# Block differences moved from GpSimd to VectorE, and a hand-written order made anew with other costs

## Chip, core and metric

The kernel runs on one core of one Trainium2 chip. The metric is the device time of one execution in microseconds (us); the median of three runs counts. Engines are called by their short names: PE (TensorE), DVE (VectorE), ACT (ScalarE), POOL (GpSimd) and SP (the queue that issues every DMA here).

## What is computed

```python
# q, k, v: (8, 8, 576, 64): attention inside chunks of 64 tokens, per head
scores = (q_c @ k_c^T) / 8; attn = softmax(scores); x = attn @ v_c
x = x as 4608 tokens x 512
h = relu(x @ moe_w_in)            # 512 x 2048
x = (h * h) @ moe_w_out           # 2048 x 512
gate = sigmoid(x @ moe2_w_gate); val = x @ moe2_w_val      # 512 x 1536 each
out = (gate * val) @ moe2_w_out   # 1536 x 512
```

All weights come as float64 and are made float32 on the chip.

## The kernel before

All four products are done in float32 exactness by three passes of a reduced format: each operand is split into a high part (one ACT copy) and a low part (one DVE subtraction, line 447, `out = value - high`, both in SBUF). Each 2x2 block product is done in Strassen's manner with seven products P1 to P7 instead of eight, so operands are first subtracted from each other. The order of the program is:

1. Attention of 36 tiles of 128 tokens (lines 816 to 914) beside the product with w_in: matmuls of line 649 with 384 columns.
2. The product with w_out (line 1031, 384 columns), class `Long`: for each of six token pairs the seven products, each over eight weight groups. For one group PE does six matmuls; ahead of it stand one low-part subtraction on DVE and, in P5, P6, P7 and P4, one block subtraction (line 456) of the tiles `g` that were loaded from DRAM.
3. The products with w_gate and w_val (line 649, 512 and 256 columns).
4. The last product (line 1031, 512 and 256 columns), class `Long` again, over six weight groups, with tiles `u` in place of `g`.

Class `Long` takes a table `engines` that says for each of the four differences which engine does it; what the table doesn't name goes to POOL:

```python
for oo, xx, yy in zip(o, x, y):
    binary(self.engines.get(p, "POOL"), self.words(oo), self.words(xx), self.words(yy), ALU.subtract,
           self.n, [oo], {oo, xx, yy})
```

Weights are prepared on the way (lines 489 to 512 turn float64 into float32: two steps on ACT, three on DVE at lines 496, 498 and 505, and one addition on POOL at line 512; `wf` and `w` are such weights). Sums of weight blocks (`ws`, `sums`) and differences of token blocks of products 1 and 3 (`raw`, `yr`) are POOL's, line 456.

Nothing of this stands in the order in which it is written. Every piece is a job with an engine, a cost, its inputs and outputs; class `Plan` walks through time with these costs, gives out SBUF space and PSUM banks, takes on each engine the ready job with the earliest due time, and emits the instructions in the order that it found. So a cost changes no instruction, but the place of many in each engine's queue, which is worked off in order. A job marked `shared` is one whose DVE or POOL instruction has its inputs in SBUF alone. `cost(eng, n)` gives the cost of one instruction over n columns; the table `TIMES` gives, for each attention tile, when its PE steps (turning k and q, scores S, turning T, mixing X) are due.

## Time and profile before

| | us |
|---|---|
| median of 3 runs (1633.62 to 1635.81) | 1635.25 |
| the profiled execution | 1635.46 |
| its span, first to last instruction | 1633.7 |
| PE busy | 1599.7 (98%) |
| DVE busy | 1376.7 (84%) |
| ACT busy | 974.6 (60%) |
| POOL busy | 817.1 (50%) |

The profile is of one execution; 1.8 us of its time lie outside the span. An engine counts as busy from the start of an instruction's record to its end, so time in which an instruction is held up by another engine counts as busy too.

### The profile page before, as it was taken

To read this page: it belongs to the slowest core of one execution; us is meant where nothing else is said; L and a number is where in the kernel's file an instruction comes from. 1 tells how busy PE (TensorE), PEld (TensorE's weight loads), DVE (VectorE), ACT (ScalarE), POOL (GpSimd) and SP (SyncE) were. 2 spreads that over 40 slices of the span, in tenths; PEclk is the share of its full clock that TensorE was granted. 3 is DMA by queue.
4 is the path that set the end of the run, shared out by engine and by line. 5 is a ranking of instruction groups with operands and counts; after the bars stand their busy time and mean duration, and the time that the engine had idled before them with its cause. 6 is when DMAs were issued, how large, how long until landed. Compare 5 with 4: busy or idle time off the path is not lost.

```text
span 1633.7 us, 30814 instructions
## 1 busy us (share of the span) xinstructions
PE 1599.7 (98%) x10500; PEld 1445.2 (88%) x10500; DVE 1376.7 (84%) x2074; ACT 974.6 (60%) x1968; POOL 817.1 (50%) x636
## 2 busy tenths in 40 slices
PE   7999999999999999999999999999999999999998
PEld 5998998999899999999997898888888888877887
DVE  7998877788889999999999796755777858799996
ACT  7876666676676566565565565544555545545543
POOL 1253403030534544544479695644666647387672
PEclk8999999999999999999999999999999999999999
DMA  9864565877884665685687746487536578866572
GB/s 229 224 184 131 143 182 151 214 196 219 265 274 153 224 204 181 197 260 182 214 274 243 273 148 217 168 282 265 185 138 243 186 248 253 273 194 159 162 179 46
DMA packets 390798, 333.36 MB, mean 204 GB/s; under 512 B 234736, under 2 KB 325616, under 8 KB 390640
## 3 DMA queue, kind: packets, MB, share of 16 engines
q1 hardware_dynamic: 390640, 331.38, 66.5%
q8 instruction: 83, 1.36, 0.4%
q14 instruction: 75, 0.61, 0.1%
HBM read 209.13 MB, written 122.16 MB: 203 GB/s over the span
## 4 chain that ended last, share of the span: by engine, by line
PE 84%; DVE 9%; DMA 2%; issue 2%; ACT 1%; POOL 1%; SPq 1%; DVEq 0%; POOLq 0%; ACTq 0%
PE bank L649 46%; PE bank L1031 35%; PE bank L836 1%; PE bank L816 1%; PE bank L896 1%; DMA wraw__1337<-in_moe_w_in_dram 1%; PE bank L880 1%; SPq L420 1%; DMA gd<-c__4078 0%; DMA v__9966<-ad 0%; DMA k__299<-in_k_dram 0%; POOL ws__7533 L456 0%; DMA k__4752<-in_k_dram 0%; POOL wf__7203 L512 0%; DMA ud<-s__10228 0%
## 5 line engine op out<-in xcount | busy, mean ns | idle before, releaser
L512 POOL TENSOR_TENSOR wf__3400<-wf__3400,wr__3217 128x512 int32<-128x512 int32 x16 | 21.9, 1372 | 160.5 <-DVE wf__3400 L505 56.3
L512 POOL TENSOR_TENSOR wf__7203<-wf__7203,wr__6924 128x512 int32<-128x512 int32 x18 | 25.3, 1406 | 88.0 <-DVE wf__7203 L505 19.6
L512 POOL TENSOR_TENSOR wf__7000<-wf__7000,wr__6924 128x512 int32<-128x512 int32 x18 | 27.2, 1510 | 62.2 <-DVE wf__7000 L505 38.9
L456 POOL TENSOR_TENSOR raw__510<-raw__679,raw__510 128x384 f32<-128x384 f32 x20 | 24.4, 1240 | 55.6 <-DVE B__640 L447 23.3
L493 ACT ACTIVATE wr__6924<-wr__6924 128x512 int32<-128x512 uint32 x36 | 23.8, 662 | 0.0
L447 DVE TENSOR_TENSOR wx__7711<-ws__7533,wx__7711 128x512 fp32r<-128x512 f32 x18 | 17.7, 983 | 3.3 <-ACT wx__7711 L442 3.3
L447 DVE TENSOR_TENSOR wx__7143<-ws__7533,wx__7143 128x512 fp32r<-128x512 f32 x18 | 18.6, 1035 | 0.3 <-ACT wx__7143 L442 0.3
L496 DVE TENSOR_SCALAR wf__7203<-wf__7203 128x512 f32<-128x512 f32 x18 | 9.9, 549 | 9.6 <-ACT wf__7203 L489 9.6
L498 DVE TENSOR_SCALAR wf__7203<-wf__7203 128x512 int32<-128x512 int32 x18 | 17.4, 968 | 0.6
L489 ACT ACTIVATE wf__3400<-wr__3217 128x512 f32<-128x512 f32 x16 | 10.7, 666 | 11.3 <-DMA wf<-wf__3400 11.3
L456 POOL TENSOR_TENSOR ws__7533<-wf__7000,wf__7203 128x256 f32<-128x256 f32 x18 | 16.5, 915 | 1.3 <-DVE wx__7711 L447 1.1
L456 POOL TENSOR_TENSOR ws__7533<-ws__7533,wf__7000 128x256 f32<-128x256 f32 x18 | 15.8, 877 | 1.2
L512 POOL TENSOR_TENSOR w__670<-w__670,wraw__566 128x512 int32<-128x512 int32 x1 | 1.3, 1289 | 29.5 <-DMA wraw__645<-in_moe_w_in_dram 29.5
L447 DVE TENSOR_TENSOR wx__7485<-wf__7203,wx__7485 128x256 fp32r<-128x256 f32 x18 | 13.3, 737 | 3.1 <-ACT wx__7485 L442 3.1
L496 DVE TENSOR_SCALAR wf__7000<-wf__7000 128x512 f32<-128x512 f32 x18 | 9.8, 544 | 6.2 <-ACT wf__7000 L489 6.2
L498 DVE TENSOR_SCALAR wf__7000<-wf__7000 128x512 int32<-128x512 int32 x18 | 14.2, 791 | 0.6
L505 DVE SCALAR_TENSOR_TENSOR wf__7203<-wr__6924,wf__7203 128x512 int32<-128x512 int32 x18 | 14.5, 807 | 0.2
L489 ACT ACTIVATE wf__7000<-wr__6924 128x512 f32<-128x512 f32 x18 | 11.9, 660 | 4.3 <-POOL ws__7533 L456 4.3
L505 DVE SCALAR_TENSOR_TENSOR wf__7000<-wr__6924,wf__7000 128x512 int32<-128x512 int32 x18 | 13.5, 752 | 0.1
L914 ACT ACTIVATE raw__679<-bank 128x256 f32<-128x256 f32 x36 | 11.8, 384 | 2.4 <-PE bank L896 2.2
L456 POOL TENSOR_TENSOR raw__510<-raw__510 128x384 f32<-128x384 f32 x10 | 13.2, 1338 | 0.0
L489 ACT ACTIVATE wf__7203<-wr__6924 128x512 f32<-128x512 f32 x18 | 11.8, 657 | 1.3 <-DMA wr__6924<-in_moe_w_val_dram 1.2
(5901 smaller groups left out, 6470.2 us busy)
## 6 DMA issues: line engine op xcount, KB each, us to landing
ad<-wx__7143 SPq DMA_DIRECT2D x27, 512.0 KB, 4.2
ad<-wx__7711 SPq DMA_DIRECT2D x27, 512.0 KB, 4.6
wr__3217<-in_moe_w_out_dram SPq DMA_DIRECT2D x16, 512.0 KB, 4.3
wr__6924<-in_moe_w_gate_dram SPq DMA_DIRECT2D x12, 512.0 KB, 4.6
wr__6924<-in_moe_w_val_dram SPq DMA_DIRECT2D x12, 512.0 KB, 4.4
wr__6924<-in_moe_w_out_dram SPq DMA_DIRECT2D x12, 512.0 KB, 4.1
ad<-wx__7485 SPq DMA_DIRECT2D x18, 256.0 KB, 4.6
wf<-wf__3400 SPq DMA_DIRECT2D x16, 256.0 KB, 4.4
```

Of the source, the lines that this page charges most:

```text
L420: nc.sync.dma_start(out=a, in_=b)
L447: lambda: nc.vector.tensor_tensor(out=lo(), in0=at(src, n, F32, off), in1=hi().bitcast(F32), op=ALU.subtract),
L456: eng, cost(eng, n), lambda: e.tensor_tensor(out=o(), in0=a(), in1=b(), op=op),
L489: nc.scalar.activation(out=at(w), in_=t[:, :, 1].bitcast(F32), func=ACTF.Abs)
L493: nc.scalar.activation(out=low, in_=low.bitcast(U32), func=ACTF.Copy, scale=2.0**-29)
L496: nc.vector.tensor_scalar_max(at(w), at(w), TINY)
L498: nc.vector.tensor_scalar(out=wi, in0=wi, scalar1=5, scalar2=2, op0=ALU.logical_shift_left, op1=ALU.logical_shift_right,)
L505: nc.vector.scalar_tensor_tensor(out=wi, in0=words()[:, :, 1], scalar=-0x40000000, in1=wi, op0=ALU.bitwise_and, op1=ALU.bitwise_or,)
L512: nc.gpsimd.tensor_tensor(out=wi, in0=wi, in1=words()[:, :, 0], op=ALU.add)
L649: nc.tensor.matmul(out=o, lhsT=at(op, P, F32R, wi * size + half * HB + kk * P), rhs=at(xb, n, F32R, xi * xsize + off), start=(first and kk ...
L816: nc.tensor.transpose(out=at(ps, P, F32, hp * P), in_=at(r, P, F32, hp * P), identity=ident)
L1031: nc.tensor.matmul(out=at(ps[m], n), lhsT=at(w, P, F32R, wi * size + half * HB + m * P), rhs=at(x, n, F32R, xi * n), start=(first and kp = ...
```

## The change

Three things are edited. The `engines` tables of products 2 and 4 now name DVE for all four differences. The planner's rule for jobs that share a port is replaced: it had charged a DVE job part of the rest of a POOL job and a POOL job a tenth, and now it has one time, `port`, until which the port is taken, for jobs of both engines. And the costs of ACT, DVE and POOL instructions are set lower, with new due times in 30 of the 36 rows of `TIMES` (two of them stand here).

```diff
-        port = {"DVE": 0.0, "POOL": 0.0, "debt": 0.0}
+        port = 0.0
...
                 elif j.shared and j.eng == "DVE":
-                    cost += port["debt"] + min(0.82 * cost, 0.45 * max(0.0, port["POOL"] - t))
-                    port["debt"], port["DVE"] = 0.0, t + cost
+                    port = max(t, port) + cost
+                    cost = port - t
                 elif j.shared:
-                    cost += 0.1 * min(cost, max(0.0, port["DVE"] - t))
-                    port["debt"] += 0.45 * min(cost, max(0.0, port["DVE"] - t))
-                    port["POOL"] = t + cost
+                    port = max(t + self.AHEAD, port) + cost - self.AHEAD
+                    cost = port - t
...
+    AHEAD = 0.15
...
-        per = {"ACT": (0.17, 0.0009), "DVE": (0.1, 0.00115), "POOL": (0.3, 0.0024)}[eng]
+        per = {"ACT": (0.07, 0.0009), "DVE": (0.06, 0.00106), "POOL": (0.16, 0.00213)}[eng]
...
-        job("DVE", 0.95, three, [w], [w], shared=True)
-        job("DVE", 0.7, four, [raw, w], [w], shared=True)
-        job("POOL", 1.4, five, [raw, w], [w], shared=True)
+        job("DVE", 0.8, three, [w], [w], shared=True)
+        job("DVE", 0.61, four, [raw, w], [w], shared=True)
+        job("POOL", 1.27, five, [raw, w], [w], shared=True)
...
-        (69.25, None, 51.5, 67.5, 72.25),
+        (64.25, None, 63, 73.5, 74.5),
...
-        (276.25, None, 275.5, 291, 289),
+        (273, None, 283.25, 286.75, 289.25),
...
-            (lambda s=s: Long(w1out, blocks_g(s), BL1, per1, finish_y(s), {"P5": "DVE", "P6": "DVE"})) for s in range(pairs1)
+            (lambda s=s: Long(w1out, blocks_g(s), BL1, per1, finish_y(s), {"P5": "DVE", "P6": "DVE", "P7": "DVE", "P4": "DVE"})) for s in range(pairs1)
...
-                              per if len(s) == 2 else per_h, finish3(s), {}))
+                              per if len(s) == 2 else per_h, finish3(s), {"P5": "DVE", "P6": "DVE", "P7": "DVE", "P4": "DVE"}))
```

The number of instructions stays what it was; 216 of them go from POOL to DVE: 96 of 384 columns in product 2, and 96 of 512 and 24 of 256 columns in product 4. The order moves on every engine. Three places are shown. In these rows a name like `x_14336__14935` is tile `x`, its address and the number that the trace gives it too.

First place: DVE in the last product, about where the trace of before stands at 1446 us. `x` is a split operand, `u` a loaded token block. Before:

```order
L447 TENSOR_TENSOR x_14336__14935<-u_133120__14572,x_14336__14935 128x512
L447 TENSOR_TENSOR x_22528__14552<-u_126976__14622,x_22528__14552 128x512
L447 TENSOR_TENSOR x_18432__14599<-u_137216__14332,x_18432__14599 128x512
L447 TENSOR_TENSOR x_10240__14712<-u_43008__14821,x_10240__14712 128x512
L447 TENSOR_TENSOR x_14336__14935<-u_45056__14839,x_14336__14935 128x512
L447 TENSOR_TENSOR x_55296__14528<-u_0__14594,x_55296__14528 128x512
L447 TENSOR_TENSOR x_67584__15259<-u_61440__15078,x_67584__15259 128x512
L447 TENSOR_TENSOR x_71680__15271<-u_198656__14170,x_71680__15271 128x512
L447 TENSOR_TENSOR x_22528__14552<-u_8192__15014,x_22528__14552 128x512
L447 TENSOR_TENSOR x_18432__14599<-u_59392__15025,x_18432__14599 128x512
```

After the change, at the same split of this product (the 64th of 512 columns):

```order
L456 TENSOR_TENSOR u_61440__14291<-u_61440__14291,u_22528__14217 128x512
L447 TENSOR_TENSOR x_96256__14902<-u_55296__14708,x_96256__14902 128x512
L447 TENSOR_TENSOR x_34816__15088<-u_0__14188,x_34816__15088 128x512
L447 TENSOR_TENSOR x_133120__15008<-u_14336__14993,x_133120__15008 128x512
L447 TENSOR_TENSOR x_137216__15275<-u_6144__14170,x_137216__15275 128x512
L456 TENSOR_TENSOR u_16384__15241<-u_16384__15241,u_83968__14678 128x512
L447 TENSOR_TENSOR x_129024__14928<-u_18432__14794,x_129024__14928 128x512
L456 TENSOR_TENSOR u_43008__14808<-u_43008__14808,u_67584__14688 128x512
L456 TENSOR_TENSOR u_22528__14217<-u_22528__14217,u_69632__14698 128x512
L447 TENSOR_TENSOR x_75776__14512<-u_20480__14757,x_75776__14512 128x512
L456 TENSOR_TENSOR u_124928__15263<-u_124928__15263,u_55296__14708 128x512
```

Before, one split stands behind the other, and the block differences that they read are POOL's; after the change five of eleven rows are these differences.

Second place: DVE in the first pairs of the product with w_out, about 494 us. `g` is a loaded token block, `e` a result in PSUM that is added. Before:

```order
L456 TENSOR_TENSOR g_53760__6217<-g_114688__6451,g_53760__6217 128x384
L447 TENSOR_TENSOR wot_186368__6528<-ws_79872__5842,wot_186368__6528 128x512
L447 TENSOR_TENSOR x_198656__6435<-g_204800__6406,x_198656__6435 128x384
L456 TENSOR_TENSOR g_7680__6227<-g_105984__6456,g_7680__6227 128x384
L447 TENSOR_TENSOR x_201728__6449<-g_104448__6411,x_201728__6449 128x384
L447 TENSOR_TENSOR x_100352__6454<-g_24576__6431,x_100352__6454 128x384
L456 TENSOR_TENSOR g_40448__6245<-g_6144__6485,g_40448__6245 128x384
L447 TENSOR_TENSOR x_194048__6372<-g_62976__6438,x_194048__6372 128x384
```

After the change:

```order
L456 TENSOR_TENSOR g_44032__6222<-g_167424__6465,g_44032__6222 128x384
L456 TENSOR_TENSOR g_17920__6233<-g_13824__6475,g_17920__6233 128x384
L447 TENSOR_TENSOR x_189440__6383<-g_32256__6206,x_189440__6383 128x384
L447 TENSOR_TENSOR x_52224__6509<-g_44032__6222,x_52224__6509 128x384
L456 TENSOR_TENSOR g_19456__6242<-g_168960__6490,g_19456__6242 128x384
L447 TENSOR_TENSOR x_84992__6522<-g_17920__6233,x_84992__6522 128x384
L456 TENSOR_TENSOR g_50688__6257<-g_1536__6336,g_50688__6257 128x384
L447 TENSOR_TENSOR x_23040__6624<-g_19456__6242,x_23040__6624 128x384
L456 TENSOR_TENSOR e_79872__6556<-e_79872__6556,bank_76 128x384
L456 TENSOR_TENSOR e_112640__6558<-e_112640__6558,bank_78 128x384
L456 TENSOR_TENSOR g_16384__6271<-g_170496__6511,g_16384__6271 128x384
L447 TENSOR_TENSOR x_4608__6354<-g_50688__6257,x_4608__6354 128x384
```

Here P5's differences (g from g) were on DVE before as well; what is gone from beside them are P7's (`b12 = b22 - b12`), which POOL did from 500 us on, and a split of a weight sum (`wot`) has left this stretch.

Third place: POOL and DVE where the first product goes to its last pair of token blocks, from 417 us. `raw` holds tokens, `T` and `B` are their split operands, `wf` a weight of product 2. POOL before:

```order
L456 TENSOR_TENSOR raw_6144_94208__510<-raw_6144_88064__679,raw_6144_94208__510 128x384 x2
L512 TENSOR_TENSOR wf_165888__3400<-wf_165888__3400,wr_18432__3217 128x512
L456 TENSOR_TENSOR raw_6144_94208__510<-raw_6144_88064__679,raw_6144_94208__510 128x384 x2
L456 TENSOR_TENSOR raw_6144_88064__679<-raw_6144_88064__679 128x384 x2
L456 TENSOR_TENSOR raw_6144_94208__510<-raw_6144_94208__510 128x384 x2
```

POOL after:

```order
L456 TENSOR_TENSOR raw_6144_94208__501<-raw_6144_88064__677,raw_6144_94208__501 128x384 x4
L456 TENSOR_TENSOR raw_6144_88064__677<-raw_6144_88064__677 128x384 x2
L456 TENSOR_TENSOR raw_6144_94208__501<-raw_6144_94208__501 128x384 x2
```

DVE before:

```order
L447 TENSOR_TENSOR B_3072_198656__760<-raw_6144_94208__510,B_3072_198656__760 128x384
L456 TENSOR_TENSOR b_12288__2870<-b_12288__2870,bank_73 128x384
L456 TENSOR_TENSOR e_6144__3147<-e_6144__3147,bank_79 128x384
L1131 SCALAR_TENSOR_TENSOR b_12288__2870<-b_12288__2870 128x384
L456 TENSOR_TENSOR c_43008__2745<-c_43008__2745,bank_76 128x384
L1131 SCALAR_TENSOR_TENSOR e_6144__3147<-e_6144__3147 128x384
L496 TENSOR_SCALAR wf_165888__3400<-wf_165888__3400 128x512
L498 TENSOR_SCALAR wf_165888__3400<-wf_165888__3400 128x512
L505 SCALAR_TENSOR_TENSOR wf_165888__3400<-wr_18432__3217,wf_165888__3400 128x512
L447 TENSOR_TENSOR T_3072_195584__789<-raw_6144_94208__510,T_3072_195584__789 128x384
L447 TENSOR_TENSOR T_3072_192512__799<-raw_6144_94208__510,T_3072_192512__799 128x384
L456 TENSOR_TENSOR b_30720__5684<-b_30720__5684,bank_75 128x384
```

DVE after:

```order
L447 TENSOR_TENSOR B_3072_198656__668<-raw_6144_94208__501,B_3072_198656__668 128x384
L1131 SCALAR_TENSOR_TENSOR e_55296__2287<-e_55296__2287 128x384
L456 TENSOR_TENSOR b_16384__2446<-b_16384__2446,bank_72 128x384
L1131 SCALAR_TENSOR_TENSOR b_16384__2446<-b_16384__2446 128x384
L456 TENSOR_TENSOR c_40448__2926<-c_40448__2926,bank_78 128x384
L447 TENSOR_TENSOR T_3072_195584__768<-raw_6144_94208__501,T_3072_195584__768 128x384
L447 TENSOR_TENSOR T_3072_192512__781<-raw_6144_94208__501,T_3072_192512__781 128x384
L456 TENSOR_TENSOR e_32256__2524<-e_32256__2524,bank_75 128x384
L1131 SCALAR_TENSOR_TENSOR e_32256__2524<-e_32256__2524 128x384
L456 TENSOR_TENSOR b_6144__4956<-b_6144__4956,bank_79 128x384
L447 TENSOR_TENSOR T_3072_189440__1983<-raw_6144_94208__501,T_3072_189440__1983 128x384
L447 TENSOR_TENSOR T_3072_186368__1990<-raw_6144_94208__501,T_3072_186368__1990 128x384
```

The POOL addition of `wf` that stood between the differences of `raw`, and the three DVE steps of `wf` between the `B` and the `T` splits, have gone to other places.

## Rows read from the trace of the kernel before

**Rows 1.** The page: span, and busy us (share of the span) of each engine.
```profile
span 1633.7 us, 30814 instructions
...
PE 1599.7 (98%) x10500; PEld 1445.2 (88%) x10500; DVE 1376.7 (84%) x2074; ACT 974.6 (60%) x1968; POOL 817.1 (50%) x636
```

**Rows 2.** Stretches: us; PE, PEld, DVE, ACT, POOL busy (instructions); clock; DMA share; GB/s.
```profile
128.00:140.00 12.00, 9.79 (x49) 8.76 (x48) 11.61 (x18) 6.15 (x14) 6.36 (x6) 0.86 0.17 45
...
266.00:276.00 10.00, 7.51 (x34) 7.19 (x33) 8.82 (x15) 4.63 (x10) 5.57 (x5) 0.83 0.54 198
...
428.00:437.00 9.00, 6.64 (x30) 5.91 (x29) 7.79 (x11) 6.55 (x15) 5.90 (x7) 0.81 0.94 323
...
500.00:516.00 16.00, 13.86 (x73) 12.12 (x72) 16.00 (x21) 6.35 (x14) 10.70 (x9) 1.00 0.21 68
516.00:831.00 315.00, 315.00 (x1817) 314.82 (x1817) 305.86 (x477) 190.54 (x390) 147.61 (x115) 1.00 0.64 205
831.00:905.00 74.00, 72.97 (x334) 61.04 (x333) 72.85 (x83) 49.03 (x90) 59.38 (x39) 1.00 0.78 267
...
1362.00:1446.00 84.00, 84.00 (x372) 69.55 (x371) 73.53 (x78) 43.52 (x73) 54.21 (x36) 1.00 0.80 233
1446.00:1492.00 46.00, 45.36 (x179) 31.80 (x178) 46.00 (x39) 20.80 (x36) 38.98 (x23) 1.00 0.65 189
1492.00:1626.00 134.00, 134.00 (x710) 116.06 (x709) 124.86 (x160) 66.42 (x135) 80.39 (x60) 1.00 0.56 141
```

**Rows 3.** Waits of PE: waited for what, us in total, times, longest.
```profile
PE bank L649 <- DVE b__3715 L456: 2.5, 1, 2.5
PE bank L649 <- DVE T__2024 L447: 2.1, 2, 1.9
PE bank L880 <- DVE a__1976 L873: 2.0, 1, 2.0
```

**Rows 4.** Timeline in the last product: start, us, engine, line, out<-in [idle before].
```profile
1447.41 1.86 PE L1031 MATMUL bank<-x__14599,o__14531 128*128 128x512 f32 x6
1447.43 1.74 POOL L456 TENSOR_TENSOR u__14436<-u__14170,u__14436 128x512 f32<-128x512 f32 x1
1447.94 1.77 DVE L447 TENSOR_TENSOR x__14712<-u__14821,x__14712 128x512 fp32r<-128x512 f32 x1
...
1449.10 1.86 PE L1031 MATMUL bank<-x__14712,o__14583 128*128 128x512 f32 x6
...
1449.64 1.77 DVE L447 TENSOR_TENSOR x__14935<-u__14839,x__14935 128x512 fp32r<-128x512 f32 x1
```

**Rows 5.** Timeline of DVE in the last product, POOL at rest.
```profile
1469.70 0.68 DVE L447 TENSOR_TENSOR x__15382<-u__14481,x__15382 128x512 fp32r<-128x512 f32 x1
1470.31 0.68 DVE L447 TENSOR_TENSOR x__15322<-u__15225,x__15322 128x512 fp32r<-128x512 f32 x1
```

**Rows 6.** Timeline of DVE in the product with w_out.
```profile
488.48 0.55 DVE L447 TENSOR_TENSOR x__6435<-g__6292,x__6435 128x384 fp32r<-128x384 f32 x1
488.94 0.55 DVE L447 TENSOR_TENSOR x__6449<-g__6304,x__6449 128x384 fp32r<-128x384 f32 x1
...
502.07 1.36 DVE L447 TENSOR_TENSOR x__6603<-g__6217,x__6603 128x384 fp32r<-128x384 f32 x1
503.35 1.37 DVE L447 TENSOR_TENSOR x__6506<-g__6227,x__6506 128x384 fp32r<-128x384 f32 x1
```

**Rows 7.** Timeline of DVE, last change of token blocks in the first product.
```profile
420.99 1.24 DVE L496 TENSOR_SCALAR wf__3400<-wf__3400 128x512 f32<-128x512 f32 x1
...
424.49 1.66 DVE L447 TENSOR_TENSOR T__799<-raw__510,T__799 128x384 fp32r<-128x384 f32 x1
```

**Rows 8.** Timeline of DVE ahead of the wait at 267 us.
```profile
264.92 0.71 DVE L759 STREAM_TRANSPOSE qT__3773<-ql__3653 128x512 f32<-128x512 f32 x1 [2.29 <-DMA gd<-e__2302]
```

**Rows 9.** Waits of POOL for loads in the last product.
```profile
POOL u__14797 L456 <- DMA u__14641<-ud: 10.5, 1, 10.5
POOL u__14641 L456 <- DMA u__14641<-ud: 9.7, 1, 9.7
```

More of the change, by code (lines that the diff above doesn't have):

```diff
@@ L196, in begin @@
         def begin(j):
-            nonlocal dma, done, shift, small
+            nonlocal dma, done, shift, small, port
             j.start, j.started = t, True
@@ L512, in five @@
             nc.gpsimd.tensor_tensor(out=wi, in0=wi, in1=words()[:, :, 0], op=ALU.add)
-        job("ACT", 0.66, one, [raw], [w], look=look)
-        job("ACT", 0.66, two, [raw], [raw])
-        job("DVE", 0.95, three, [w], [w], shared=True)
-        job("DVE", 0.7, four, [raw, w], [w], shared=True)
-        job("POOL", 1.4, five, [raw, w], [w], shared=True)
+        job("ACT", 0.56, one, [raw], [w], look=look)
+        job("ACT", 0.56, two, [raw], [raw])
+        job("DVE", 0.8, three, [w], [w], shared=True)
+        job("DVE", 0.61, four, [raw, w], [w], shared=True)
+        job("POOL", 1.27, five, [raw, w], [w], shared=True)
         return w
@@ L759, in go @@
                 nc.vector.transpose(out=y, in_=x)
-            job("DVE", 0.1 + 0.15 * n, go, [r], [o])
+            job("DVE", 0.04 + 0.15 * n, go, [r], [o])
             i += n
@@ new lines, in tile_attention_relu2_glu @@
+        (158.5, None, 163.5, 167, 183.5),
+        (182.75, None, 185.25, 192.5, 190.25),
+        (192.25, None, 192.5, 200, 194.75),
+        (197.25, None, 199.5, 203.25, 209),
+        (194.75, None, 201.5, 203.25, 200),
+        (205.25, None, 211.25, 219.75, 219.75),
+        (216.5, None, 225.25, 234.75, 229),
+        (247, None, 242.75, 254.5, 261.5),
+        (259.5, None, 253.75, 269.25, 275.25),
+        (268, None, 259, 267.5, 273.25),
+        (266.5, None, 264.25, 282.75, 290),
+        (272.75, None, 262.5, 277.25, 291),
@@ L861, in attention @@
         for c in range(2):
[L862 removed]
+            job("DVE", 0.34, lambda c=c: nc.vector.tensor_reduce(
                 out=largest(c), in_=chunk(c), axis=AX.X, op=ALU.max), [ps_s[c]], [mx])
[L864 removed]
+            job("DVE", 0.34, lambda c=c: nc.vector.tensor_tensor(
                 out=of_chunk(c), in0=chunk(c), in1=largest(c).to_broadcast([P, HP, CH]), op=ALU.subtract),
                 [ps_s[c], mx], [a])
[L867 to L868 removed]
+        job("ACT", 0.53, lambda: nc.scalar.activation(out=at(a), in_=at(a), func=ACTF.Exp, scale=scale), [a], [a])
+        job("DVE", 0.6, lambda: nc.vector.tensor_reduce(out=col8(mx, 1), in_=heads(a), axis=AX.X, op=ALU.add), [a], [mx])
         def norm():
@@ L916, in attention @@
         for c in range(2):
-            job("ACT", 0.37, lambda c=c: put(c), [ps_x[c]], [raw])
+            job("ACT", 0.27, lambda c=c: put(c), [ps_x[c]], [raw])
     def add(o, a, b, n, ob, ib):
@@ L1340, in finish @@
                 o = sbuf(n, "o")
-                job("DVE", 0.1 + 0.00118 * n, lambda: nc.vector.transpose(out=at(o), in_=at(t)), [t], [o], soon=2.0)
+                job("DVE", 0.06 + 0.00106 * n, lambda: nc.vector.transpose(out=at(o), in_=at(t)), [t], [o], soon=2.0)
                 t0 = s[col] * BLK if len(s) == 2 else col * HB
```

50 lines of the change are left out of this document (17 added, 33 removed).

## Prediction

> **What bounds the kernel now.** The page comes first [rows 1]: PE is busy 1599.7 of 1633.7 us, so the time is PE's work plus the little that PE loses. The second view is the table of stretches [rows 2], in which the losses can be placed. Where PE runs undisturbed it does 1817 matmuls of 384 columns in 315 us, 0.1734 us each, and 372 of 512 columns in 84 us, 0.2258 us each. By these prices 46 us from 1446 us on hold 179 matmuls, which is 40.4 us of work: 5.6 us are lost although PE counts as busy for 45.4. From 500 to 516 us 73 matmuls are 12.7 us of work: 3.3 us lost. In the first product three short stretches stand out, at 128, 266 and 428 us: PE is idle there for 2.2, 2.5 and 2.4 us, and the granted clock is 0.86, 0.83 and 0.81 of full speed, which over 12, 10 and 9 us takes another 1.7 us from each. At half of 2.4 GHz PE does half the work, so each of these waits costs about 4.1 us, 12.1 together. The clock falls behind a wait of some 2 us and is whole again a few us on. From 831 to 905 us PE is idle for 1.0 us.
>
> The third view, the waits of PE, says what ended these [rows 3]: DVE each time. So the question is what makes DVE late, and the timeline answers it. In the last product at 1447 us a split on DVE takes 1.77 us and the next starts 1.70 later, beside POOL differences of 1.74 us, and PE does six matmuls each 1.69 us, not 1.36 [rows 4]. Twenty us later, with POOL at rest, the same split takes 0.68 us and the next starts 0.61 later [rows 5]. With 384 columns the two cases are 1.28 and 0.46 us from start to start [rows 6]. So one POOL instruction holds a DVE instruction up for about 1.09 us at 512 columns and 0.82 at 384. Busy time of DVE, 97% in some stretches [rows 2], is in good part such holding.
>
> **The differences in the last product.** One wide pair is 42 steps of six matmuls, 56.9 us of PE. Before, DVE has 42 splits, 6 additions and 8 transposes at 0.61 (34.2 us) and is held up 24 times for 1.09 (26.2): 60.4 us, more than PE needs. That is why PE goes at DVE's pace at 1447 us; work done ahead keeps the loss to 5.6. After the change the 24 differences cost DVE 24 x 0.61 = 14.6, in sum 48.8 of 56.9 us. In a step with a difference DVE needs 2 x 0.61 = 1.22 us against PE's 1.36. No transpose is known to be held up and the trace has no block difference of 512 columns on DVE; the split, an operation of the same kind, shape and operands, is the nearest row, and a difference at 0.61 stays the likely price. It would take 0.95 for a pair to become DVE's again ((56.9 - 34.2) / 24), and at nothing the sum wouldn't change, since PE bounds the rest. The first place of the order shows what this costs in the queue: differences stand among the splits and additions now. The cover is PE's own time in this stage; if it is gone, each 0.1 us of a difference costs 120 x 0.1 = 12 us at most. Of the 5.6 us I take 5.5, between nothing and 5.6.
>
> **The differences in the product with w_out.** A pair is 56 steps, 58.3 us of PE. DVE before: 56 splits, 16 differences and 6 additions at 0.46 (35.9) and 16 delays of 0.82 (13.1): 49.0. After: 94 instructions, 43.2. So DVE gains 5.8 us a pair for weights, which both versions prepare here. The loss at 500 us comes as POOL's P7 differences hold up P5's on DVE; in the second place of the order those have gone. Sums of weights stay on POOL and can still delay a split. I take 3.0 of 3.3, with zero as the other end.
>
> **The first product.** No difference moves here, only the order. At 428 us the path was: three `wf` steps on DVE, the first held to 1.24 us, then a `T` split of 0.46, then one held to 1.66 [rows 7] while POOL did `wf` between the `raw` differences. In the third place of the order both are gone from there and four `raw` differences follow each other. From the first `wf` step to the second `T` split are 3.5 us; without the 0.46 of the first split the steps that left are 3.0, more than PE's wait of 2.4: I take the whole 4.1. At 266 us DVE had itself been idle for 2.29 us, for a load, and stood with a transpose ahead of the splits [rows 8]; such transposes of `q` stand ahead of the splits in the new order too, so the load decides. At 128 us the last step of a softmax came late [rows 3]; differences and softmax tails of this kind still meet in the new order. For these two I take half, 4.05, between 0 and 8. The same order brings waits of its own that no row can show: between none and three of 4.1; since the due times follow costs near the measured 0.46 and 0.61 better than those of before, I take 1.2, near the lower end. ACT's, PE's and the DMAs' work is the same in number. From 831 to 905 us five weights fewer are left to prepare in products 3 and 4 (22 instead of 27 by the order): I take 0.6 of the 1.0, between 0 and 1.0. The start and the last 8 us I leave as they are: the number of DVE steps ahead of the first matmul of w_in is 57 before and 58 after, between 1 us gained and lost.
>
> **Sum.** -5.5 - 3.0 - 4.1 - 4.05 + 1.2 - 0.6 = -16.05. The profiled execution took 1635.46 us, 0.2 over the median of the runs: 1619.4, so 1619.
>
> **Rivals.** *More goes*: all losses named go and no new wait comes: -5.6 - 3.3 - 12.1 - 1.0 = -22.0, 1613, and some of the smaller waits of the first product with them. For it: DVE has less to do and less delay in each stage. Against it: a chip's loads land late now and then, whatever the order.
>
> *No gain*: products 2 and 4 gain their 9.1 but the first product keeps its 12.1 and gets two waits more, 8.2: 1635.46 - 9.1 + 8.2 = 1634.6. For it: 30 rows of due times are new and each PE wait above 2 us costs twice its length.
>
> *Slower, by late loads*: the differences read tiles that come from DRAM. POOL waited for them, 10.5 and 9.7 us in the last product [rows 9], and nothing else stood behind it. DVE works its queue in order: if a difference waits there, splits and the additions that free PSUM banks wait too. Splits are made about 5 us ahead (the planner's `look=5.0`), so a wait counts from 5 us on: 5.5 + 4.7, and 1.7 of clock for each, 13.6 us; as much again in the product with w_out makes 27: 1619 + 27 = 1646. Against it: POOL was there early because it had nothing else to do, and the planner puts a difference in line only when it expects the load.
>
> *Slower, DVE becomes the bound*: DVE is busy 244.4 of 264 us in the last product and 305.9 of 315 in w_out [rows 2]. If this were work, 120 differences (96 x 0.61 and 24 x about half) add 66 and 96 x 0.46 add 44, which overruns by 46 and 35 us: 1635 + 81 = 1716. Rows 4 and 5 speak against it, as much of this busy time is delay by the very instructions that go. The Trainium skill has a rule of this kind: its page "Perfetto Trace Analysis", section "Optimizing Scalar/DVE Operations", says that with DVE saturated, handing work to ScalarE or even GpSimd may make sense, and adds that between DVE and GpSimd it might not help, as they share a read port of SBUF. By its first half this change goes the wrong way; the trace agrees with its second half (0.68 us alone, 1.77 beside POOL).
>
> **Chances.** The forecast 0.55 (1613 to 1629), more 0.20, no gain 0.11, late loads 0.10, DVE the bound 0.02, other new waits in the first product that outweigh all 0.02. A change under 0.2% (3.3 us) can't be told from none here. So faster 0.75, same 0.11, slower 0.14. The range is 1606 to 1637: below lies a quarter of the second case, above it the slower ones.
>
> **What would show it.** In the profile after: splits of 512 columns in the last product at 0.68 us throughout, no POOL work there, PE at 0.2258 us a matmul from 1362 us on; DVE busy for about 222 us of it (168 splits, 96 differences and 56 additions and transposes at 0.61 are 195, 85 narrow ones at half 26), less than now. In w_out no stretch with a matmul above 0.1734 us after the first pair. In the first product at most one granted clock below full after 40 us. The prediction is wrong if DVE waits for loads of `g` or `u`, or if PE waits for DVE above 2 us in three or more places of the first product.

## The result, and the profile after

The changed kernel takes 1620.70 us (median of 4 runs, 1619.29 to 1623.55) against 1635.53 of the kernel before in the same job: a ratio of 0.9913, with a 95% interval of 0.9896 to 0.9930. Faster, by 14.8 us.

The page after, span and busy times as in [rows 1]:

```profile
span 1621.5 us, 30663 instructions
...
PE 1590.0 (98%) x10500; PEld 1442.0 (89%) x10500; DVE 1325.2 (82%) x2290; ACT 971.5 (60%) x1968; POOL 524.8 (32%) x420
```

PE is busy for 9.7 us less with the same matmuls, so it was held up less; POOL lost 292 us of work and DVE, which took over 216 instructions, is busy for 51 us *less*.

The place of the gain is read from stretches that begin where a product begins (first 34 us, product 1 with the attention, w_out, product 3, last product with the last stores). The kernel before, columns as in [rows 2]:

```profile
0.00:33.40 33.40, 23.98 (x461) 18.44 (x461) 22.45 (x56) 22.20 (x43) 1.99 (x7) 0.93 1.09 230
33.40:487.90 454.50, 441.18 (x4248) 421.00 (x4245) 384.31 (x725) 315.74 (x690) 140.40 (x127) 0.98 0.71 199
487.90:841.30 353.40, 351.25 (x2018) 349.34 (x2018) 343.87 (x528) 213.84 (x441) 172.00 (x136) 1.00 0.64 208
841.30:1361.80 520.50, 519.26 (x2522) 438.62 (x2521) 380.72 (x493) 291.21 (x551) 328.93 (x250) 1.00 0.64 220
1361.80:1633.70 271.90, 263.99 (x1261) 217.79 (x1259) 245.40 (x277) 131.60 (x244) 173.78 (x118) 0.99 0.64 175
```

After, and three short stretches at the places of the waits at 128, 266 and 428 us in [rows 2]:

```profile
0.00:34.00 34.00, 23.47 (x469) 18.00 (x469) 23.21 (x56) 22.79 (x46) 2.09 (x7) 0.95 1.09 218
34.00:484.70 450.70, 438.14 (x4237) 416.55 (x4238) 377.51 (x724) 311.88 (x692) 139.59 (x127) 0.99 0.72 200
484.70:834.10 349.40, 349.40 (x2017) 349.40 (x2016) 341.07 (x650) 225.34 (x460) 78.18 (x57) 1.00 0.70 231
834.10:1355.40 521.30, 520.09 (x2523) 438.73 (x2522) 360.01 (x470) 278.58 (x530) 303.28 (x229) 1.00 0.63 213
1355.40:1621.50 266.10, 258.91 (x1262) 219.37 (x1260) 223.44 (x394) 132.90 (x244) 1.67 (x2) 0.99 0.61 166
126.00:142.00 16.00, 13.42 (x125) 12.49 (x115) 11.56 (x25) 8.01 (x20) 1.33 (x2) 0.89 0.39 101
276.00:290.00 14.00, 11.74 (x61) 11.38 (x60) 11.08 (x24) 7.37 (x17) 3.35 (x4) 0.88 0.60 197
414.00:430.00 16.00, 16.00 (x150) 15.68 (x150) 12.71 (x20) 12.56 (x31) 10.04 (x9) 1.00 0.83 271
```

Stage by stage, after less before: +0.6, -3.8, -4.0, +0.8, -5.8, in sum the -12.2 us between the two spans. (The profiled execution of the changed kernel, 1623.55 us, is the longest of its four, so the medians differ by 2.6 us more than these spans do.) In w_out PE counts as busy in all of the 349.4 us and DVE has 650 instructions in less busy time than 528 had before. Of product 1 the stretch where the 428 us wait stood is clean; the other two waits have successors of the same size, at 131 and 278 us, with clocks of 0.89 and 0.88.

Waits of PE in the changed kernel, columns as in [rows 3]:

```profile
PE bank L649 <- ACT aT__2078 L427: 2.6, 1, 2.6
PE bank L649 <- DVE b__3816 L456: 2.3, 1, 2.3
PE bank L649 <- ACT c__3765 L427: 1.3, 1, 1.3
```

DVE in the last product, timeline as in [rows 4, 5], at the rows that the first place of the order shows:

```profile
1439.52 0.69 DVE L447 TENSOR_TENSOR x__15275<-u__14170,x__15275 128x512 fp32r<-128x512 f32 x1
1440.12 0.69 DVE L456 TENSOR_TENSOR u__15241<-u__15241,u__14678 128x512 f32<-128x512 f32 x1
1440.73 0.69 DVE L447 TENSOR_TENSOR x__14928<-u__14794,x__14928 128x512 fp32r<-128x512 f32 x1
1441.33 0.69 DVE L456 TENSOR_TENSOR u__14808<-u__14808,u__14688 128x512 f32<-128x512 f32 x1
1441.93 0.69 DVE L456 TENSOR_TENSOR u__14217<-u__14217,u__14698 128x512 f32<-128x512 f32 x1
```

Block differences (`u` from `u`) and splits (`x`) alternate; each has a record of 0.69 us and the next starts 0.60 to 0.61 later, the price of [rows 5]. POOL does 1.67 us of work in this whole stage.

### The profile page after: what moved, and what is told of

It reads as the page before. It is cut to its first block, busy times and chain, and to the rows that moved or that the text cites. A ratio compares the mean times of both kernels' runs of the same rounds, so it can differ in the third digit from the quotient of the medians.

```text
span 1621.5 us, 30663 instructions
## 1 busy us (share of the span) xinstructions
PE 1590.0 (98%) x10500; PEld 1442.0 (89%) x10500; DVE 1325.2 (82%) x2290; ACT 971.5 (60%) x1968; POOL 524.8 (32%) x420
## 4 chain that ended last, share of the span: by engine, by line
PE 73%; DVE 2%; issue 1%; POOL 1%; ACT 0%; DMA 0%; SPq 0%; DVEq 0%; POOLq 0%; ACTq 0%
PE bank L1031 37%; PE bank L649 35%; PE bank L896 0%; PE bank L836 0%; DMA w__5725<-wf 0%; POOL ws__5872 L456 0%; POOL ws__5810 L456 0%; DVE T__1990 L447 0%; PE bank L880 0%; DMA g__6317<-gd 0%; POOL ws__7199 L456 0%; DVE T__1983 L447 0%; DVE b__4956 L456 0%; ACT c__3874 L427 0%; POOL wf__7139 L512 0%
## 5 line engine op out<-in xcount | busy, mean ns | idle before, releaser
L512 POOL TENSOR_TENSOR wf__6765<-wf__6765,wr__6689 128x512 int32<-128x512 int32 x18 | 36.4, 2023 | 170.0 <-DVE wf__6765 L505 52.7
L512 POOL TENSOR_TENSOR wf__3460<-wf__3460,wr__3365 128x512 int32<-128x512 int32 x16 | 21.5, 1341 | 172.5 <-DVE wf__3460 L505 65.9
L512 POOL TENSOR_TENSOR wf__7139<-wf__7139,wr__6689 128x512 int32<-128x512 int32 x18 | 28.0, 1558 | 115.4 <-DVE wf__7139 L505 73.6
L496 DVE TENSOR_SCALAR wf__7139<-wf__7139 128x512 f32<-128x512 f32 x18 | 11.9, 659 | 7.0 <-ACT wf__7139 L489 7.0
L496 DVE TENSOR_SCALAR wf__6765<-wf__6765 128x512 f32<-128x512 f32 x18 | 11.5, 641 | 6.1 <-ACT wf__6765 L489 6.0
L442 ACT ACTIVATE wx__7204<-wf__7139 128x256 fp32r<-128x256 f32 x18 | 7.4, 413 | 12.2 <-POOL wf__7139 L512 12.2
L496 DVE TENSOR_SCALAR wf__3460<-wf__3460 128x512 f32<-128x512 f32 x16 | 7.3, 456 | 8.5 <-ACT wf__3460 L489 7.2
L427 ACT ACTIVATE c__12027<-bank 128x512 f32<-128x512 f32 x8 | 4.8, 597 | 14.0 <-PE bank L649 14.0
L498 DVE TENSOR_SCALAR wf__6765<-wf__6765 128x512 int32<-128x512 int32 x18 | 12.6, 698 | 0.6
```

What stands on the lines that cost most here:

```text
L427: lambda: nc.scalar.activation(out=o(), in_=i(), func=func, **kw), ib, ob, soon=soon,
L442: lambda: nc.scalar.activation(out=hi(), in_=at(src, n, F32, off), func=ACTF.Copy),
L496: nc.vector.tensor_scalar_max(at(w), at(w), TINY)
L498: nc.vector.tensor_scalar(out=wi, in0=wi, scalar1=5, scalar2=2, op0=ALU.logical_shift_left, op1=ALU.logical_shift_right,)
L512: nc.gpsimd.tensor_tensor(out=wi, in0=wi, in1=words()[:, :, 0], op=ALU.add)
```

## Experiments

Each experiment is given by its edit; "the stages" are those of the table above, always from its own trace. "Weights early" are the weight blocks of product 3, of 36, whose integer step on DVE (line 505) stands in the w_out stage: 9 before, 14 after.

### What the move is worth alone, and what the order

The kernel before with the two `engines` tables alone changed:

```diff
-  ... finish_y(s), {"P5": "DVE", "P6": "DVE"} ...
+  ... finish_y(s), {"P5": "DVE", "P6": "DVE", "P7": "DVE", "P4": "DVE"} ...
...
-  ... finish3(s), {} ...
+  ... finish3(s), {"P5": "DVE", "P6": "DVE", "P7": "DVE", "P4": "DVE"} ...
```

> The kernel before with its old costs, old port rule and old due times; only the two engine tables name VectorE for all four differences. The order of VectorE is that of before up to its row 838, so the first product is untouched. Theory A (GpSimd instructions hold up VectorE, and moving the differences takes that away): the 5.6 us lost in the last product and most of the 3.3 us lost from 500 to 516 us go: 1635.5 - 5.5 - 3.0 = 1627. Rival B (the gain came from the new order alone, and the moved work costs VectorE as much as it saves): 1634 to 1637. Rival C (all of the gain came from the move): 1621.

Measured: 1638.55 us, ratio 1.0022 (1.0012 to 1.0032). The move alone gains nothing. That is close to rival B's 1634 to 1637, but not for B's reason: products 2 and 4 gain 4.0 and 4.9 us, near the 3.0 and 5.5 that were forecast for them:

```profile
486.90:836.30 349.40, 349.40 (x2017) 349.40 (x2017) 325.78 (x616) 214.25 (x436) 40.25 (x34) 1.00 0.62 201
836.30:1367.20 530.90, 523.50 (x2522) 440.25 (x2521) 390.34 (x503) 296.37 (x557) 328.40 (x252) 0.99 0.64 220
1367.20:1634.20 267.00, 259.23 (x1262) 219.31 (x1260) 224.72 (x395) 134.43 (x244) 1.26 (x2) 1.00 0.66 182
```

Product 3, in which no difference moved, goes from 520.5 to 530.9 us and takes it all back: PE is idle there for 7.4 us against 1.2, and the granted clock of its first 100 us is 0.97, which is about 3 us more. Its longest wait of PE, 2.9 us for the split of `T__10273`, and the timeline that led there:

```profile
862.36 1.40 DVE L498 TENSOR_SCALAR wf__7153<-wf__7153 128x512 int32<-128x512 int32 x1
...
863.44 1.47 POOL L456 TENSOR_TENSOR yr__9996<-yr__9996,yr__9960 128x512 f32<-128x512 f32 x1
...
864.28 1.17 DVE L505 SCALAR_TENSOR_TENSOR wf__7153<-wr__7081,wf__7153 128x512 int32<-128x512 int32 x1
...
865.68 1.27 POOL L512 TENSOR_TENSOR wf__7153<-wf__7153,wr__7081 128x512 int32<-128x512 int32 x1 [0.78 <-ACT T__10088 L442]
865.98 1.53 DVE L447 TENSOR_TENSOR T__10273<-yr__10018,T__10273 128x512 fp32r<-128x512 f32 x1
...
867.56 0.79 PE L649 MATMUL bank<-T__10273,g__9872 128*128 128x512 f32 x1 [2.92 <-DVE T__10273 L447]
```

Two steps of a weight (`wf`, lines 498 and 505) stand ahead of the split on DVE and take 1.40 and 1.17 us beside POOL's differences; in the changed kernel's w_out stage they take 0.43 and 0.69 on average. The split itself takes 1.53 beside POOL's integer addition. It is the holding of [rows 4] again, one stage later. Only 7 weights were early, so 29 were left for product 3, against 27 before and 22 after.

The opposite: the changed kernel with the old `engines` tables, so that only the order is new.

```diff
-  ... finish_y(s), {"P5": "DVE", "P6": "DVE", "P7": "DVE", "P4": "DVE"} ...
+  ... finish_y(s), {"P5": "DVE", "P6": "DVE"} ...
...
-  ... finish3(s), {"P5": "DVE", "P6": "DVE", "P7": "DVE", "P4": "DVE"} ...
+  ... finish3(s), {} ...
```

> The changed kernel with the differences back where they were (P7 and P4 of w_out and all four of the last product on GpSimd); new costs, port rule and due times stay, and VectorE's order is that of the changed kernel up to its row 846, so the first product is that of the changed kernel. Theory A: the losses of the last product and of w_out come back, about 5.5 + 3.0: 1629; the gain of the first product, some 3 us by its end in the two traces, stays. Rival B (the order alone): 1621. Rival C (the move alone): 1635.

Measured: 1633.74 us, ratio 0.9996 (0.9985 to 1.0006), near rival C's 1635.

```profile
481.60:840.20 358.60, 353.30 (x2017) 348.98 (x2017) 344.64 (x539) 216.43 (x447) 184.88 (x140) 1.00 0.66 216
...
1361.90:1629.70 267.80, 260.58 (x1262) 218.86 (x1260) 250.45 (x277) 133.26 (x243) 178.19 (x120) 0.99 0.61 168
```

w_out takes 358.6 us, 5.2 longer than before, with waits of PE for splits (1.4 us the longest), the last product 267.8. So neither part pays alone; the 14 us exist only together.

The changed kernel with the last product's table alone put back:

```diff
-  ... finish3(s), {"P5": "DVE", "P6": "DVE", "P7": "DVE", "P4": "DVE"} ...
+  ... finish3(s), {} ...
```

> The changed kernel with the differences of the last product alone back on GpSimd. Its order is that of the changed kernel until close to the last product. Theory A: that product again goes at 1.70 us a step where a difference stands beside a split, and 5.5 us are lost: 1626; from the first to the last matmul of the last product 264 us in place of 259. Rival B (the planner now knows the port and puts the differences where they don't hurt): 1621 to 1623.

Measured: 1624.41 us, ratio 0.9941 (0.9928 to 0.9953), between theory A's 1626 and rival B's 1621 to 1623.

```profile
1354.70:1624.10 269.40, 261.61 (x1262) 218.51 (x1260) 249.53 (x277) 134.61 (x244) 176.74 (x119) 0.99 0.61 165
```

The last product takes 269.4 us against 266.1, and w_out and product 3 don't move (349.4 and 521.1). In the new order the move of 120 differences is worth 3.3 us there; against the run before this one, where the same differences are POOL's too, it is 1.7; in the old order (271.9 to 267.0) it was worth 4.9. The rest of the 5.8, 0.9 to 4.1, comes from the order.

### Which part of the new planner is needed

The changed kernel whose jobs on DVE and POOL know nothing of each other:

```diff
                 elif j.shared and j.eng == "DVE":
-                    port = max(t, port) + cost
-                    cost = port - t
+                    pass
+                    pass
...
                 elif j.shared:
-                    port = max(t + self.AHEAD, port) + cost - self.AHEAD
-                    cost = port - t
+                    pass
+                    pass
```

> The changed kernel, but its planner charges nothing for the shared port; costs, due times and engine tables stay. The order differs from VectorE's row 60 on. Theory D (an order that knows of the port keeps GpSimd instructions out of VectorE's tight places in the first product): one to three more waits with a drop of the clock there, 4.1 us each: 1625 to 1633. Rival E (the costs and due times do it, the rule itself changes nothing that can be measured): 1619 to 1623.

Measured: 1707.16 us, ratio 1.0437 (1.0418 to 1.0456): product 1 473.9, w_out 369.8, product 3 561.4, the last 266.6. That is far above both forecasts: the rule is worth 86 us, in w_out and product 3 as well as in the first product. The three stages in which DVE and POOL work side by side are all longer; the last, where POOL rests, is not.

Then the three parts were added to the move one by one. First the new numbers of `cost` alone, with the old rule and due times:

```diff
-        per = {"ACT": (0.17, 0.0009), "DVE": (0.1, 0.00115), "POOL": (0.3, 0.0024)}[eng]
+        per = {"ACT": (0.07, 0.0009), "DVE": (0.06, 0.00106), "POOL": (0.16, 0.00213)}[eng]
```

> The move of the differences with the old port rule and old due times, but with the new numbers in the function cost(): 13 of the 36 weights of products 3 and 4 are prepared before product 3, where the move alone had 7. Theory F (with the old, too dear costs the planner held VectorE for full during w_out, left the weights for product 3, and there they collide with GpSimd's differences; this ate the gain of the move): product 3 takes 521 us in place of 531, in sum 1628, give or take 4 for the first product, whose order changes too. Rival G (product 3 was slow for another reason): product 3 stays at 531, in sum 1638.

Measured: 1665.39 us, ratio 1.0177 (1.0163 to 1.0191). Both theories of this run fell: product 3 is neither at 521 nor at 531.

```profile
33.20:501.80 468.60, 442.81 (x4244) 420.92 (x4245) 381.33 (x725) 316.15 (x691) 136.07 (x123) 0.98 0.68 190
...
854.30:1396.70 542.40, 524.71 (x2522) 438.99 (x2522) 366.49 (x472) 282.99 (x534) 306.95 (x234) 1.00 0.60 206
```

The longest waits of PE in product 3 are now for additions and copies that free PSUM banks, not for splits:

```profile
PE bank L649 <- DVE b__10885 L456: 2.5, 3, 1.5
PE bank L649 <- DVE b__10174 L456: 2.5, 2, 1.6
PE bank L649 <- ACT c__10284 L427: 2.4, 1, 2.4
```

The rule alone on top of the move, with the old costs and due times (the whole edit of the rule stands in "The change"):

```diff
-        port = {"DVE": 0.0, "POOL": 0.0, "debt": 0.0}
+        port = 0.0
...
+                    port = max(t, port) + cost
+                    cost = port - t
...
+                    port = max(t + self.AHEAD, port) + cost - self.AHEAD
+                    cost = port - t
...
+    AHEAD = 0.15
```

> The kernel before with the differences of w_out and of the last product on VectorE and with the rule that a float operation of GpSimd is put only where VectorE has nothing placed; the planner's engine costs, engine times and attention times stay as before. 6 of the 36 weight blocks are written before product 3. Theory A (the rule alone keeps GpSimd's work out of VectorE's tight places, and the move then pays): w_out 349.4, product 3 back at about 521, last product 266 to 267, the time about 1624 to 1630. Theory B (too few weights are ready when product 3 starts, whatever the rule): product 3 at 530 to 536 as in the move alone, the time 1636 to 1642.

Measured: 1664.62 us, ratio 1.0191 (1.0175 to 1.0206); product 1 463.7, product 3 541.6.

```profile
852.80:1394.40 541.60, 525.20 (x2522) 437.15 (x2522) 389.68 (x508) 297.28 (x560) 329.88 (x254) 1.00 0.62 215
```

Both theories of that run fell: the rule alone does harm, and far more than the weights explain (seven are early by the trace; the move alone has seven too, and 530.9).

Rule and costs together, both diffs above on top of the move, due times still the old ones:

> As the run before it, with the new engine costs in the planner as well; engine times of the ordering and attention times as before. 13 of the 36 weight blocks are written before product 3. Theories A and B both allow 1622 to 1632 here. Theory C (the lower costs pack VectorE too tightly as long as the old engine times and attention times set the places): the first product is 10 us or more longer, as where the costs were changed without the rule (501.8 for everything up to w_out), and the time is over 1635.

Measured: 1627.06 us, ratio 0.9950 (0.9936 to 0.9964).

```profile
36.40:492.70 456.30, 442.39 (x4242) 421.93 (x4241) 382.04 (x726) 313.84 (x691) 137.82 (x127) 0.98 0.71 196
492.70:842.10 349.40, 349.40 (x2017) 349.40 (x2017) 336.27 (x643) 222.04 (x454) 69.09 (x53) 1.00 0.68 225
842.10:1360.90 518.80, 518.36 (x2522) 438.94 (x2521) 353.27 (x474) 282.66 (x534) 306.13 (x233) 1.00 0.61 209
1360.90:1626.60 265.70, 258.99 (x1262) 219.45 (x1261) 222.28 (x395) 134.06 (x244) 1.30 (x2) 1.00 0.67 182
```

Products 2 to 4 are as good as in the changed kernel or better (349.4, 518.8, 265.7); only product 1 is longer, 456.3 against 450.7, and its start 2.4. So the new due times, with the job costs edited beside them, are worth the 6.4 us from 1627.06 to 1620.70: 8.0 in the first stage by the traces, of which product 3 gives 2.5 back. With the old due times the four combinations stand so:

| | old rule | new rule |
|---|---|---|
| old numbers of `cost` | 1638.55 | 1664.62 |
| new numbers of `cost` | 1665.39 | 1627.06 |

So each needs the other; that is shown. Why is argued from the numbers: the new ones give a DVE operation of 512 columns 0.60 and a POOL one 1.25, close to the pitch of [rows 5] and the 1.27 of POOL's addition in the timeline above, and the new rule then queues one behind the other. The old numbers, 0.69 and 1.53, are above those, so with the new rule the holding would be counted twice, and with the new numbers and the old rule too little. The changed kernel with only its old rule, only its old costs or only its old due times was not tried.

### Weights early

The changed kernel, in which the loads of the first half of product 3's weights may start later or earlier (`LK` is how many us ahead of the due time):

```diff
-        LK = 260.0, 500.0
+        LK = 60.0, 500.0
```

> The changed kernel, but the loads of the first half of the gate and value weights may start only 60 us ahead of their due time in place of 260: 6 of the 36 weights are prepared before product 3 in place of 14; VectorE's order is the same up to its row 856. Theory F: product 3 loses 5 to 10 us more, 1626 to 1631. Rival G: nothing changes, 1621.

Measured: 1638.84 us, ratio 1.0015 (1.0007 to 1.0024). Six weights are early instead of 14.

```profile
836.30:1371.70 535.40, 524.10 (x2522) 438.59 (x2521) 394.49 (x511) 299.69 (x567) 333.84 (x255) 1.00 0.65 222
```

w_out takes 351.0 and product 3 535.4, 14.1 more than after and more than the 5 to 10 of theory F. In the first 100 us of product 3 DVE is busy for 93.0 us, against 81.1 in the changed kernel; PE's waits in the product, none above 1.8 us, are mostly for splits on DVE, but one of 1.8 is for a prepared weight that comes back from DRAM (`v__10793`). So in this order weights that come late cost 14 us. Their number does not settle it: 7 early go with 530.9 and 541.6 us (the move alone, with the new rule), 9 with 520.5 (before), 11 with 521.7 (the order alone), 13 with 542.4 and 518.8 (the new costs alone, rule and costs).

And the other way:

```diff
-        LK = 260.0, 500.0
+        LK = 400.0, 500.0
```

> The changed kernel with these loads allowed 400 us ahead: 34 of the 36 weights are prepared before product 3. Theory F: product 3 loses almost nothing, 2 to 4 us less than now: 1617 to 1619, if w_out can carry 20 more weights (by 1.5 us of VectorE and 1.1 of GpSimd's hold each, 52 us, where some 60 to 90 are free). Rival H (w_out becomes VectorE's): 1625 or more.

Measured: 1889.98 us, ratio 1.1555 (1.1534 to 1.1576), nearly all of it by one wait:

```profile
PE bank L1031 <- ACT wos__7278 L442: 260.0, 1, 260.0
```

The high-part copy of a sum of w_out's own weights (`wos`) came behind 34 weights of product 3: from 515 to 776 us DVE did the integer steps of all 34. That is over rival H's 1625, but not because w_out became VectorE's; its order did it. Product 3 then took 518.8 us without a weight to prepare, 2.5 less than after; rule and costs with the old due times took 518.8 with 23 weights still to do.

### Would DVE become the bound

The changed kernel, in which the low-part subtraction of P5, P6, P7 and P4 in the last product is done twice with the same result (120 instructions more on DVE):

```diff
+                if self.again and p in ("P5", "P6", "P7", "P4"):
+                    c = min(n, self.again)
+                    job(
+                        "DVE", cost("DVE", c),
+                        lambda x=x, r=r, c=c: nc.vector.tensor_tensor(
+                            out=at(x, c, F32R, n), in0=at(r, c), in1=at(x, c, F32R).bitcast(F32), op=ALU.subtract
+                        ),
+                        [r, x], [x], shared=True,
+                    )
...
-  ... finish3(s), {"P5": "DVE", "P6": "DVE", "P7": "DVE", "P4": "DVE"}))
+  ... finish3(s), {"P5": "DVE", "P6": "DVE", "P7": "DVE", "P4": "DVE"}, 512))
```

> The changed kernel, with the low-part subtraction of the last product done twice where a difference is made (P5, P6, P7, P4; same values, 120 more VectorE instructions). It prices VectorE's room in the last product. By 0.61 us an instruction a wide pair needs 48.8 + 24 x 0.61 = 63.4 us of VectorE against 56.9 of TensorE: 26 us over four pairs and some 5 for the narrow one, less the work done ahead (about 8 us): 1636 to 1650. Rival I (VectorE has far more room, so that the move cost nothing because the price was wrong): under 1625.

Measured: 1649.85 us, ratio 1.0083 (1.0070 to 1.0097), at the top of the forecast range.

```profile
1353.20:1647.50 294.30, 272.71 (x1261) 217.15 (x1259) 283.95 (x514) 131.55 (x244) 1.57 (x2) 0.99 0.56 150
```

A wide pair now needs 104 x 0.61 = 63.4 us of DVE against 56.9 of PE: 6.5 more, 26 us over the four wide pairs, about 23 by the expectation with the narrow pair and the work done ahead; the stage grew by 28.2, from 266.1 to 294.3. So the working by the price of an instruction that is alone holds to within some 5 us beyond the point where DVE becomes the bound, and by it the change stays 8 us a pair short of that point.

### More of the same

The changed kernel with the token differences of products 1 and 3 on DVE, and, in a second kernel, also the weight sums and gate products (the last two edits):

```diff
         def minus(o, x, y):
             for oo, xx, yy in zip(o, x, y):
-                binary("POOL", part(oo), part(xx), part(yy), ALU.subtract, n, [oo[0]], {oo[0], xx[0], yy[0]})
+                binary("DVE", part(oo), part(xx), part(yy), ALU.subtract, n, [oo[0]], {oo[0], xx[0], yy[0]})
...
-                binary("POOL", part(*o), part(*x), part(*y), op, HB, [sums],
+                binary("DVE", part(*o), part(*x), part(*y), op, HB, [sums],
...
-                    binary("POOL", u.words(gate), u.words(t), u.words(gate), ALU.mult, n, [gate], [gate, t], soon=4.0)
+                    binary("DVE", u.words(gate), u.words(t), u.words(gate), ALU.mult, n, [gate], [gate, t], soon=4.0)
```

> The changed kernel with the token differences of products 1 and 3 on VectorE too: 107 differences more leave GpSimd. By the price that the two engines pay when both work (a difference of 384 columns 0.46 on VectorE alone, 0.98 to 1.25 on GpSimd with VectorE held for as long) VectorE's queue gets shorter in products 1 and 3 and part of the 33 and 4 us lost there comes back: 1614 to 1619. Rival 1 (these differences lie beside idle VectorE, nothing to gain): 1619 to 1622. Rival 2 (VectorE's queue is where the waits come from, and more work in it makes them longer): 1623 to 1635.

> The changed kernel with all float differences and sums on VectorE (token differences, gate products, weight sums: 335 instructions moved); GpSimd keeps only integer additions. Port theory: VectorE's busy time goes from 1325 to about 1425 of 1621 and the time is 1612 to 1619. Rival (VectorE becomes the bound in product 1 or 3, where its own share is highest): over 1625, with waits of TensorE for VectorE in those products that the changed kernel does not have.

Measured: 1630.82 us, ratio 0.9977 (0.9967 to 0.9986), and 1632.29, ratio 0.9983 (0.9974 to 0.9992): 10 and 12 us slower than the changed kernel. The numbers are those of rival 2 and of the second run's rival, but only product 1 is longer, and DVE is busy for 1364.5 us in the second, not 1425.

```profile
34.00:495.30 461.30, 443.40 (x4239) 418.13 (x4238) 383.26 (x766) 312.90 (x692) 94.16 (x87) 0.99 0.70 194
...
844.70:1363.30 518.60, 518.12 (x2522) 438.72 (x2521) 353.57 (x541) 281.01 (x528) 182.85 (x155) 1.00 0.62 214
```

```profile
35.00:494.00 459.00, 442.15 (x4238) 418.58 (x4237) 387.77 (x821) 313.77 (x690) 42.74 (x31) 0.99 0.71 196
...
843.40:1363.10 519.70, 518.59 (x2522) 439.02 (x2521) 391.04 (x676) 282.51 (x530) 30.64 (x22) 1.00 0.62 214
```

Product 3 gains 2.7 and 1.6 us, and DVE does not become the bound in it. That the price of contention gives this gain is not shown, as rule and costs with the old due times took 518.8 us there with these differences on POOL. Product 1 loses 10.6 and 8.3. Its longest waits are not for the moved differences: in the first of the two PE waits 2.8 us for a copy on ACT, at 269 us, in the second 5.0 us for a transpose of `q` on DVE, at 148 us. Both end a chain that begins on SP (below). They are not the whole loss: PE is idle in the stage for 17.9 and 16.9 us, against 12.6 in the changed kernel, and some of the gaps are small. What makes up the rest stays open, and whether due times made for these orders would give it back was not tried.

## Why the prediction came out as it did

**The last product** (-5.5): the stage went from 271.9 to 266.1, -5.8. The splits keep 0.69 us throughout, POOL is at rest, PE takes no loss, and DVE is busy for 223.4 us where 222 were forecast. Mechanism and size hold; the experiments add that 0.9 to 4.1 us of it are the order's and not the move's.

**The product with w_out** (-3.0): -4.0. All of the loss went, with the move alone too (349.4 us); 0.7 of it had lain outside the stretch from 500 to 516 us. The delays by sums of weights on POOL, for which 0.3 was kept back, cost nothing.

**The first product** (-4.1 at 428 us, -4.05 for half of two others, +1.2 for new waits: -6.95): -3.8, or -3.2 with the start, in the two profiled executions. The wait at 428 us went as forecast. The step that failed is the half of the waits at 128 and 266 us: in this trace both came again, at 131 and 278 us, at the same price (2.6 and 2.3 us, and 1.8 and 1.7 of clock), and with them the clock fell twice after 40 us, not once at most. Other traces of the same order, below, show that the first of the two belongs to the order and the second mostly to this execution. The reason that the prediction gave was half right. The row that it read as a load, [rows 8], names a store: `gd<-e` writes a result out (`e` is a tile in SBUF to which results from PSUM are added), and the next writer of that SBUF space waits for it (the loads of `q` that the transpose reads were issued just ahead of that store, so both hung on one queue). In the changed kernel the same happens on ACT, and the trace shows where it starts:

```profile
120.69 9.04 SPq L420 DMA_DIRECT2D ql__1500<-in_q_dram  x16
...
129.84 0.40 SPq L420 DMA_DIRECT2D gd<-e__1695  x1
...
131.98 0.49 ACT L427 ACTIVATE e__1695<-bank 128x384 f32<-128x384 f32 x1 [3.77 <-DMA gd<-e__1695]
132.36 0.52 ACT L442 ACTIVATE T__2062<-raw__501 128x384 fp32r<-128x384 f32 x1
...
133.19 0.59 ACT L427 ACTIVATE aT__2078<-bank 128x512 f32<-128x512 f32 x1
...
133.83 0.44 PE L649 MATMUL bank<-T__768,wis__1697 128*128 128x384 f32 x1 [2.58 <-ACT aT__2078 L427]
```

SP issues 16 loads of `q` one after the other, 9.04 us of its queue; the store of `e` stands behind them and is issued at 129.84. ACT's copy into `e__1695` waits for that store until 131.98 (3.8 us idle), two high-part copies and the copy of `aT` wait behind it in ACT's queue, and PE waits for `aT`. At 262 us another 16 loads of `q` hold SP for 10.12 us, and the copy to `e__3900` waits 2.8 us for a store that is issued behind them, at 273.28, and lands some 5.6 us later. In the kernel before, the store of [rows 8] was issued at 263.02 behind 16 loads of 9.46 us. So by the timelines neither DVE's load nor the port set these waits; this is argued, as spreading or moving those loads was not tried.

**Product 3** (-0.6): +0.8. Not the size but the role of this term was wrong. The prediction counted the move's gain and the order's gain as separate and let product 3 be nearly untouched. The runs show that the move alone loses 10.4 us there, and that the new rule and costs, which the prediction only weighed by the waits of the first product, give these back. The sum was near the measured 14.8 because the parts were changed together. Its closeness is in part luck as well: the terms add up to 16.05, the stages of the two profiled executions to 12.2, with the first product about 3 and product 3 1.4 us short of forecast, and the execution profiled is the longest of its four.

**The start**: +0.6, inside the bound of 1.

**The rivals.** *No gain* is what the move alone did, but by product 3 and not by new waits in product 1. (The 9.1 us that this rival gives to products 2 and 4 hold the 0.6 of product 3; the two alone were 8.5.) *Late loads*: the trace lists no wait of PE in w_out, nor in the last product up to 1614 us, and the waits of DVE that it lists there are for ACT's copies (3.7 us in four times the most) or for PE's results, not for loads. *DVE becomes the bound* fell: it took 120 instructions more to get there, as the 0.61 has it. The rule of "SBUF — State Buffer" in the Trainium skill (section "SBUF: two separate sides"), that a DVE operation with two SBUF inputs and a GpSimd operation that reads SBUF hold a shared pair of ports in turn, each for its whole length, agrees with the trace: 0.69 us alone, up to 1.77 beside POOL [rows 4].

The first stage has a spread of its own. The changed kernel and four of its variants issue the same instructions in it in the same order, and their traces differ so:

| variant | product 1, us | wait at 131 us | clock, 126 to 142 us | wait for `b__3816` at 278 us | clock, 276 to 290 us |
|---|---|---|---|---|---|
| the changed kernel | 450.7 | 2.6 | 0.89 | 2.3 | 0.88 |
| old `engines` tables | 447.6 | 2.6 | 1.00 | 0.9 | 1.00 |
| last product's table put back | 450.2 | 2.7 | 0.79 | 0.7 | 1.00 |
| weights later | 451.3 | 2.8 | 0.89 | 1.4 | 1.00 |
| split done twice | 448.5 | 2.6 | 1.00 | 1.3 | 1.00 |

The wait at 131 us is in all five, that at 278 us is long in one. And the price of a wait is not fixed: behind the same wait of 2.6 to 2.8 us the clock fell in three traces and stayed full in two, where the prediction put every such wait at twice its length. The kernel before and the move alone, whose first stages have one order too, took 454.5 and 453.7 us. By these traces the gain in the first product lies between 2.4 and 6.9 us, and single terms below 4 us there can't be settled by one trace.

## What to carry to other kernels

An operation moved from GpSimd to VectorE can make VectorE's busy time fall, if its records are long because they wait; the price to count with is the pitch of the same operation where GpSimd rests. When such a move changes a schedule, look for the stage that did not change: here the gain of 9 us in two products was lost in a third, until the planner's rule for the shared port and its costs fitted each other. A model is changed as a whole: against the move alone, its new costs alone and its new rule alone each lost some 26 us, both together gained 11.

## What was not expected of the hardware

SP's queue stood at the start of five of the long waits followed back in product 1 (one in the kernel before, two in the changed one, two in the last experiments): 16 loads of 36 KB take 8.3 to 10.1 us to issue, 0.52 to 0.63 each, while one lands a median of 2.1 us after its issue. The page "DMA: Bandwidth & Descriptors" of the Trainium skill (section "Issuing engines are not separate DMA queues") says that the time to start a DMA is usually small relative to the DMA; here one issue is a quarter to a third of a load's 2.1 us, but a row of 16 is four to five times as long as that, and what is queued behind it, a store whose issue takes 0.40, comes that much later.
